# Four gated groups of a fused attention and expert kernel computed from seven block products instead of eight

## The chip, the cores and the metric

The kernel runs on one core of a Trainium2 chip. The metric is the device time of one execution in microseconds (us). TensorE (PE) multiplies matrices, VectorE (DVE) and ScalarE (ACT) work elementwise and can read PSUM, GpSimd (POOL) works elementwise on SBUF alone, and SyncE (SP) issues most transfers.

## The reference

Random-feature attention for 2 batches of 8 heads, then a gated product, then four experts weighted by probabilities. The part that the change touches is the gated product; x has 1152 rows (2 batches of 576) and 512 columns (d_model), w1 and w2 are 512 x 1024.

```python
def _moe_ref(x, w1, w2, w3, w_out):
    a = x @ w1
    b = x @ w2
    h = a * b @ w3
    return (h @ w_out).astype(np.float32)
```

The kernel folds w3 @ w_out into one 1024 x 512 matrix beforehand, so that the gated product is followed by one product with the folded matrix. The weights come as float64 and are turned into float32 on the chip. Each float32 operand is kept as two parts, high and low (`split`: ScalarE copies the high part, another engine subtracts it from the source), and a product is made of three passes, low by high, high by low and high by high (`PASSES`).

## The kernel before

Activations stand transposed: features on the partitions, tokens along the free dimension. `xb[kk]` (kk = 0 to 3) holds 128 features of x for both batches, high and low part, 1152 columns each. It is whole only when the attention of the last heads and of the 64 tail tokens of each batch has been placed.

The gated product goes by eight groups g of 128 hidden columns. `load_w12(g)` brings the group's columns of w1 and w2: a float64 block (`load_f64` on SP's queue), its conversion to float32 (`from_f64`: one ScalarE and two VectorE instructions, into one of two buffers `w12f`), and its split into one of eight 4 KB slots of the pool `w1` (ScalarE high, GpSimd low). Groups 0 and 1 are computed for each batch by itself (`gated`), groups 2 to 7 for both batches (`gated_both`): for w1 and then w2, three thirds of 384 columns, each 4 kk x 3 passes = 12 products into one PSUM bank. ScalarE copies the three banks of w1 to SBUF (`a2`), VectorE multiplies those of w2 onto them, and the product is split into the hidden tiles of the two batches.

The order around the change is written by hand in two strings. `BESIDE` puts the fold of w3 and w_out (`fold`) and the first groups beside the attention, `AFTER` lists what follows: `wN` is `load_w12(N)`, `bBG` is `gated` for batch B and group G, `mN` is `gated_both(N)`, `cB` is `expert_input(B)`, the product of the hidden tiles with the folded matrix. Within it the Tile framework's scheduler fixes each engine's queue when the kernel is built: an instruction goes in when its inputs are expected, earlier program text first. `tc.issue_after(ins)` keeps what follows behind `ins` on that engine. The queues are then worked off in order.

`fold` accumulates a 128 x 512 piece of the folded matrix in PSUM and splits it from there into `w3o` (high and low), in the pool `w3` beside `w1` on the right-hand side of SBUF. `expert_input(b)` multiplies by `w3o`: for each half c of 288 columns, four banks of 8 kk x 3 products each. For b = 1 it also makes the sums that the experts' own seven-product scheme wants (temporaries t1, t3, b22 in the pool `xq`). The experts (`hidden`, `sums`, `second`) already use that scheme: `NAMES` gives the seven pairs of operands, `ORDER` the order of the blocks for two halves X and Y, and `combine` makes the sums of the weights. Their first weights are loaded into the two tiles of the pool `raw`.

```python
PASSES = ((LO, HI), (HI, LO), (HI, HI))
ORDER = "X1 Y1 X5 Y5 X6 Y6 X2 X7 Y2 Y7 X3 X4 Y3 Y4".split()
NAMES = {
    "1": ("A11", "B11"), "2": ("A12", "B21"), "3": ("S4", "B22"), "4": ("A22", "T4"), "5": ("S1", "T1"), "6": ("S2", "T2"),
    "7": ("S3", "T3"),
}
```

Of the kernel before, what the change touches and what calls it, by code (L numbers as in the profile page):

```python
# [39 lines left out]


BESIDE = {1: 'o o o', 2: 'o o', 3: 'o o o f0', 4: 'f1 f2', 5: 'f3 f4', 6: 'f5 f67', 7: 'w0', 8: 'b00 w1'}
AFTER = 'w2 b01 w3 b10 w4 b11 w5 m2 w6 m3 w7 m4 m5 m6 m7 c0 c1'


@with_exitstack
def attention_moe_kernel(ctx: ExitStack, tc: tile.TileContext, q, k, v, omega, mw1, mw2, mw3, mwo, probs, ew1, ew2, out):
# [110 lines left out]
    w3_p = mctx.enter_context(tc.tile_pool(name="w3", bufs=1, side="right"))  # L158
    cctx = mctx.enter_context(ExitStack())
    cv = cctx.enter_context(tc.tile_pool(name="cv", bufs=2, side="right"))  # L160
    w12, hid, wo, w3o, x2, xf = {}, {}, [], [], {}, {}

    def gated_columns(src, g):
        return src[:, g * P:(g + 1) * P].rearrange("(k p) c -> p k c", p=P)

    def load_w12(g):

        for w, src in enumerate((mw1, mw2)):
            src = gated_columns(src, g)
            with ExitStack() as order:  # L170
                if g < EARLY:
                    f = next_block("w12f")
                else:
                    with tc.issue_after(pairs[-1].loaded):
                        r = load_f64(cv.tile([P, 512, 2], U32, tag="f64", name="f64", bufs=3), [src])
                    for ins in pairs[-1].split:
                        order.enter_context(tc.issue_after(ins))
                    f = from_f64(r, "w12f")
                t = load_w64(w1_p, f, "w12", nc.gpsimd)
            w12[w, g] = t.rearrange("p a (k c) -> p a k c", k=KD)  # L180

    def load_wo():

# [3 lines left out]
    def gated(a_p, bufs, b, g, tags):  # L187

        ht = hidden_tile(b, g)
        halves = []  # L190
        for w in range(2):
            bs = [bank(tags[2 * w + c]) for c in range(2)]
            for kk in range(KD):
                for n, (x, y) in enumerate(PASSES):
                    for c in range(2):
                        nc.tensor.matmul(
                            out=bs[c][:, :HS], lhsT=w12[w, g][:, x, kk], rhs=xt[b][kk][:, y, c * HS:(c + 1) * HS],
                            start=(kk == 0 and n == 0), stop=(kk == KD - 1 and n == 2),
                        )
            for c in range(2):  # L200
                if w == 0:
                    t = a_p.tile([P, HS], F32, tag="a", name="a", bufs=bufs)
                    nc.scalar.activation(out=t, in_=bs[c][:, :HS], func=ACTF.Copy)
                    halves.append(t)
                else:
                    t, s = halves[c], slice(c * HS, (c + 1) * HS)
                    nc.vector.tensor_tensor(out=t, in0=bs[c][:, :HS], in1=t, op=ALU.mult)
                    split(ht[:, HI, s], ht[:, LO, s], t)

    def hidden_tile(b, g):  # L210
        pool = (hx_p if g < HX_BUFS else h0_p) if b == 0 else h_p
# [3 lines left out]
    def gated_both(g):  # L215

        hts = [hidden_tile(b, g) for b in range(B)]
        third = B * S // 3
        cols = [slice(c * third, (c + 1) * third) for c in range(3)]
        tags = ALL_BANKS[0] + ALL_BANKS[1]  # L220
        kept = []
        for w in range(2):
            for c in range(3):
                ps = bank(tags[(g * 6 + w * 3 + c) % 8])
                for kk in range(KD):
                    for n, (x, y) in enumerate(PASSES):
                        nc.tensor.matmul(  # L227
                            out=ps[:, :third], lhsT=w12[w, g][:, x, kk], rhs=xb[kk][:, y, cols[c]],
                            start=(kk == 0 and n == 0), stop=(kk == KD - 1 and n == 2),
                        )  # L230
                if w == 0:
                    t = a_p.tile([P, third], F32, tag="a2", name="a", bufs=4)
                    nc.scalar.activation(out=t, in_=ps[:, :third], func=ACTF.Copy)
                    kept.append(t)
                else:
                    t = kept[c]
                    nc.vector.tensor_tensor(out=t, in0=ps[:, :third], in1=t, op=ALU.mult)  # L237
                    for b in range(B):
                        lo, hi = max(c * third, b * S), min((c + 1) * third, (b + 1) * S)
                        if lo < hi:  # L240
                            s = slice(lo - b * S, hi - b * S)
                            split(hts[b][:, HI, s], hts[b][:, LO, s], t[:, lo - c * third:hi - c * third])

    w3T = []
    for n in range(KF):
# [8 lines left out]
    def fold_transposed(u):  # L254

        r = next_block("w3f")
        t = cv.tile([P, 512], U32, tag="f64e", name="w3t", bufs=2).bitcast(F32)
        nc.vector.transpose(t, r.rearrange("p (j c g) -> p j g c", j=4, g=4))  # L260
        t = t.rearrange("p (j g r) -> p g j r", j=4, g=4)
        wt = cv.tile([P, 2, 512], F32R, tag="w3T", name="w3T", bufs=2)
# [6 lines left out]
    def fold(*ms):  # L269
# [3 lines left out]
        for u, (m, hf) in enumerate(UNITS):  # L273
# [7 lines left out]
                    start=(hf == 0 and n == 0), stop=(hf == 1 and n == 11),  # L281
                )
            if hf == 1:
                t = w3_p.tile([P, 2, 512], F32R, tag="w3o", name="w3o", bufs=KF)
                split(t[:, HI], t[:, LO], sums[m])
                w3o.append(t)

    def expert_input(b):

        for c in range(2):  # L290
            s = slice(c * HS, (c + 1) * HS)
            for i in range(KD):

                j = i // 2 + i % 2 * (KD // 2)
                ps = bank(ALL_BANKS[c][i])
                for kk in range(KF):
                    for n, (x, y) in enumerate(PASSES):
                        nc.tensor.matmul(
                            out=ps[:, :HS], lhsT=w3o[kk][:, x, j * P:(j + 1) * P], rhs=hid[b, kk][:, y, s],
                            start=(kk == 0 and n == 0), stop=(kk == KF - 1 and n == 2),  # L300
                        )
                p = ps[:, :HS]
                if b == 0:
                    if c == 0:
                        new_x2(("B11", "B21")[i % 2], i // 2)
# [369 lines left out]
    raw_p = ctx.enter_context(tc.tile_pool(name="raw", bufs=2, reuse_waits="tile"))  # L675
    h_p = mctx.enter_context(tc.tile_pool(name="h", bufs=KF, reuse_waits="tile"))
    h0_p = mctx.enter_context(tc.tile_pool(name="h0", bufs=KF - HX_BUFS, reuse_waits="tile"))
    a_p = cctx.enter_context(tc.tile_pool(name="a", bufs=1, reuse_waits="tile", side="right"))
    for s in AFTER.split():
        if s[0] == "w":  # L680
            load_w12(int(s[1]))
        elif s[0] == "c":
            if s == "c0":
                cctx.close()
                xq_p = mctx.enter_context(tc.tile_pool(name="xq", bufs=1, reuse_waits="tile", side="right"))
            expert_input(int(s[1]))
        elif s[0] == "m":
            gated_both(int(s[1]))
        else:
            gated(a_p, 4, int(s[1]), int(s[2]), ALL_BANKS[int(s[1])])  # L690
    mctx.close()
# [25 lines left out]
    turn = [0]  # L717
# [5 lines left out]
    def place(o, x, y, op):  # L723
        nc.vector.tensor_tensor(out=o, in0=x, in1=y, op=op)  # L724

    def parts(t, src):
        split(t[:, HI], t[:, LO], src)
        return t

    def combine(low, high, x11, x12, x21, x22, first, both):  # L730


        t = {}
        a = both(low)
        t["A11"], t["A12"] = a[0], a[1]
        t["A22"] = first(x22)
        place(x22, x21, x22, ALU.add)
        place(x21, x11, x21, ALU.subtract)
        a = both(high)
        t["S3"], t["S1"] = a[0], a[1]  # L740
        place(x11, x22, x11, ALU.subtract)
        place(x12, x12, x11, ALU.subtract)
        a = both(low)
        t["S2"], t["S4"] = a[0], a[1]
        return t

    def raw_half(pool, src):
        r = pool.tile([P, 2, 512], F32, tag="raw", name="raw")
# [20 lines left out]
    def load_w2(hf):  # L769
# [235 lines left out]
```

## Time and profile before

| | us |
|---|---|
| median of 3 runs | 654.55 |
| lowest, highest | 653.83, 654.69 |
| the profiled execution | 654.0 |
| its span, first to last instruction | 652.2 |
| TensorE busy in the span | 640.9 |
| VectorE busy | 458.9 |
| ScalarE busy | 415.8 |
| GpSimd busy | 122.2 |

All busy times are of the one profiled execution. Busy times of different engines overlap. A matmul's own duration is longer than the distance to the next one, since matmuls are pipelined; the distance is what adds up. The same holds in small for VectorE, whose next instruction can start up to 0.1 us before the one in front of it ends.

### The profile page before, as it was taken

To read this page: it belongs to the slowest core of one execution; us is meant where nothing else is said; L and a number is where in the kernel's file an instruction comes from. 1 tells how busy PE (TensorE), PEld (TensorE's weight loads), DVE (VectorE), ACT (ScalarE), POOL (GpSimd) and SP (SyncE) were. 2 spreads that over 40 slices of the span, in tenths; PEclk is the share of its full clock that TensorE was granted. 3 is DMA by queue.
4 is the path that set the end of the run, shared out by engine and by line. 5 is a ranking of instruction groups with operands and counts; after the bars stand their busy time and mean duration, and the time that the engine had idled before them with its cause. 6 is when DMAs were issued, how large, how long until landed. Compare 5 with 4: busy or idle time off the path is not lost.

```text
span 652.2 us, 12631 instructions
## 1 busy us (share of the span) xinstructions
PE 640.9 (98%) x4971; PEld 609.3 (93%) x4971; DVE 458.9 (70%) x756; ACT 415.8 (64%) x892; POOL 122.2 (19%) x145
## 2 busy tenths in 40 slices
PE   8998999999999999999999999999999999999997
PEld 6787787799999999999999999999999999999997
DVE  4678987957533261757958968788598679687795
ACT  5899556655522242457768767688677687687750
POOL 2223000133310000000131420430422413304200
PEclk9999999999999999999999999999999999999999
DMA  9978762136200011001244782881773855836824
GB/s 249 353 175 228 168 172 66 34 97 197 64 0 1 1 69 62 1 2 65 94 127 87 111 146 51 159 147 19 149 144 51 150 108 86 141 83 95 173 57 147
DMA packets 58396, 70.61 MB, mean 108 GB/s; under 512 B 8864, under 2 KB 43680, under 8 KB 58336
## 3 DMA queue, kind: packets, MB, share of 16 engines
q1 hardware_dynamic: 44720, 48.79, 25.6%
q0 software_dynamic: 12640, 20.19, 21.1%
q8 instruction: 39, 0.64, 0.4%
q10 hardware_dynamic: 976, 0.82, 0.4%
q14 instruction: 21, 0.17, 0.1%
HBM read 47.24 MB, written 22.54 MB: 107 GB/s over the span
## 4 chain that ended last, share of the span: by engine, by line
PE 88%; ACT 5%; DMA 3%; DVE 2%; issue 1%; SPq 1%; DVEq 0%; ACTq 0%
PE ps_f L828 7%; PE ps_f L913 6%; PE ps_et L828 3%; PE ps_po L828 3%; PE ps_w L828 3%; PE ps_x L828 3%; PE ps_kv L828 3%; PE ps_t L828 3%; PE ps_et L913 3%; PE ps_x L913 3%; PE ps_kv L913 3%; PE ps_w L913 3%; PE ps_t L913 3%; DMA f<-in_moe_w_dram 3%; PE ps_po L913 3%; PE ps_f L227 3%
## 5 line engine op out<-in xcount | busy, mean ns | idle before, releaser
L862 POOL DMA_DIRECT2D out_dram<-o x98 | 82.0, 935 | 352.5 <-DVE o L888 174.0
L84 DVE TENSOR_TENSOR hs<-hd,hs 128x1024 fp32r<-128x1024 f32 x48 | 58.4, 1219 | 0.8 <-ACT hs L83 0.8
L83 ACT ACTIVATE hs<-hd 128x1024 fp32r<-128x1024 f32 x48 | 50.6, 1055 | 7.6 <-PE ps_et L913 2.5
L828 PE MATMUL ps_f<-x,w1e 128*128 128x288 f32 x288 | 46.9, 294 | 0.0
L812 ACT ACTIVATE hd<-hd 128x288 f32<-128x288 f32 x96 | 40.9, 436 | 8.0 <-DVE hd L810 7.4
L724 DVE TENSOR_TENSOR hd<-hd 128x512 f32<-128x512 f32 x64 | 43.9, 686 | 1.5 <-ACT hd L812 0.4
L724 DVE TENSOR_TENSOR raw<-raw 128x512 f32<-128x512 f32 x64 | 43.9, 686 | 0.6
L84 DVE TENSOR_TENSOR w2e<-raw,w2e 128x1024 fp32r<-128x1024 f32 x32 | 38.8, 1218 | 6.1 <-ACT w2e L83 6.0
L913 PE MATMUL ps_f<-w2e,hs 128*128 128x256 f32 x288 | 42.7, 282 | 0.0
L828 PEld LDWEIGHTS ps_f<-x,w1e 128*128 128x128 f32 x288 | 41.1, 188 | 0.2
L913 PEld LDWEIGHTS ps_f<-w2e,hs 128*128 128x128 f32 x288 | 38.2, 191 | 0.1
L83 ACT ACTIVATE w2e<-raw 128x1024 fp32r<-128x1024 f32 x32 | 32.8, 1054 | 6.1 <-DVE raw L724 3.7
L84 POOL TENSOR_TENSOR w<-w12f,w 128x512 fp32r<-128x512 f32 x16 | 21.8, 1378 | 66.9 <-ACT w L83 59.2
L84 DVE TENSOR_TENSOR w1e<-raw,w1e 128x1024 fp32r<-128x1024 f32 x24 | 29.3, 1220 | 4.4 <-ACT w1e L83 4.3
L83 ACT ACTIVATE hid<-a 128x192 fp32r<-128x192 f32 (+2 forms) x32 | 13.4, 440 | 29.1 <-DVE a L237 25.2
L83 ACT ACTIVATE w1e<-raw 128x1024 fp32r<-128x1024 f32 x24 | 25.4, 1058 | 4.6 <-DVE raw L724 2.9
L279 PE MATMUL ps_po<-wo,w3T 128*128 128x512 f32 x96 | 24.1, 399 | 1.7 <-DVE w3T L84 1.7
L381 DVE TENSOR_REDUCE mx<-ps_f 128x4 f32<-128x512 f32 x24 | 16.5, 689 | 12.5 <-PE ps_f L375 11.5
L279 PE MATMUL ps_w<-wo,w3T 128*128 128x512 f32 x96 | 24.5, 400 | 0.6 <-DVE w3T L84 0.6
L885 ACT ACTIVATE o<-ps_f,pr 128x256 f32<-128x256 f32 (+1 forms) x37 | 17.8, 480 | 10.4 <-PE ps_f L913 9.6
L84 DVE TENSOR_TENSOR hid<-a,hid 128x192 fp32r<-128x192 f32 (+2 forms) x32 | 17.5, 563 | 9.0 <-ACT hid L83 9.0
L828 PE MATMUL ps_et<-x,w1e 128*128 128x288 f32 x144 | 23.6, 295 | 0.0
(307 smaller groups left out, 1711.5 us busy)
## 6 DMA issues: line engine op xcount, KB each, us to landing
raw<-in_moe_w_dram SPq DMA_DIRECT2D x32, 512.0 KB, 5.5
out_dram<-o POOLq DMA_DIRECT2D x56, 256.0 KB, 4.7
f<-in_moe_w_dram SPq DMA_DIRECT2D x64, 128.0 KB, 3.6
f<-in_moe_w_dram SPq DMA_DIRECT2D x16, 512.0 KB, 4.3
out_dram<-o POOLq DMA_DIRECT2D x42, 128.0 KB, 5.0
f<-in_moe_w_out_dram SPq DMA_DIRECT2D x8, 512.0 KB, 7.4
vr<-in_v_dram SPq DMA_DIRECT2D x8, 256.0 KB, 5.2
o<-out_dram SPq DMA_DIRECT2D x8, 256.0 KB, 4.8
```

The costliest lines, as they stand in the source:

```text
L83: high = nc.scalar.activation(out=hi, in_=src, func=ACTF.Copy)
L84: low = (eng or nc.vector).tensor_tensor(out=lo, in0=src, in1=hi.bitcast(F32), op=ALU.subtract)
L227: nc.tensor.matmul(out=ps[:, :third], lhsT=w12[w, g][:, x, kk], rhs=xb[kk][:, y, cols[c]], start=(kk == 0 and n == 0), stop=(kk == KD - 1 ...
L279: nc.tensor.matmul(out=sums[m], lhsT=w3T[u][:, a, g * P:(g + 1) * P], rhs=wo[hf * 4 + g][:, c], start=(hf == 0 and n == 0), stop=(hf == 1 ...
L381: top = nc.vector.tensor_reduce(out=mx, in_=pv, op=ALU.max, axis=AX.X, negate=True)
L724: nc.vector.tensor_tensor(out=o, in0=x, in1=y, op=op)
L812: nc.scalar.activation(out=h, in_=src, func=ACTF.Relu)
L828: nc.tensor.matmul(out=ps, lhsT=w1t[a][:, x, kk, g * P:(g + 1) * P], rhs=x2[b, kk][:, y, s], start=(k in "125" and kk == 0 and n == 0), st ...
L862: dma = nc.gpsimd.dma_start(out=out[toks, d], in_=src[rows], **({} if fresh else dict(accum_op=ALU.add))).ins
L885: nc.scalar.activation(out=o, in_=ps, func=ACTF.Copy, scale=pr[:, t, e:e + 1])
L913: nc.tensor.matmul(out=ps, lhsT=t[a][:, x, g, j * P:(j + 1) * P], rhs=w2t[b][:, y, g], start=(k in "15" and g == 0 and n == 0), stop=(k in ...
```

## The change

Groups 4 to 7 (`WINO = 4`) are computed by the same seven-product scheme as the experts. The blocks are: w1 and w2 as the two rows, the two halves of d_model as the inner index, and the two batches as the two columns. So a group has seven block products for each half of 288 columns, each block 2 kk x 3 passes = 6 products; the sums of blocks are accumulated in PSUM and, over SBUF tiles p1, p5 and p6, on VectorE; GpSimd makes one of the two products w1 by w2.

- `sums_of_x` makes T1, T2, T3 and the float32 form of T4 from xb, in eight steps (`tN` in `AFTER`: one step for each digit) that stand beside groups 1 to 3, and `last_sum_of_x` (`t9`) splits T4 into the second half of xb[0] and xb[1], behind group 3. The float32 T4 stands in the two tiles of the pool `raw` until then.
- `load_w12_sums` makes a group's weights by `combine`: four slots of the pool `w1` instead of two.
- `fold` keeps its result as float32 (VectorE copies it out of PSUM). `split_fold` (`s0`, `s1`) splits it later into slots of the pool `w1`, four tiles behind group 6 and four behind group 7.
- `expert_input(0)` goes in its first column half through kk 0 to 3 of all four banks and then through kk 4 to 7.
- The pools on the right-hand side change their order, and `a2` has three buffers instead of four.

The pieces of the diff that carry this (the functions `combine`, `place`, `parts` and the two tables only move up in the file):

```diff
-AFTER = 'w2 b01 w3 b10 w4 b11 w5 m2 w6 m3 w7 m4 m5 m6 m7 c0 c1'
+AFTER = 'w2 b01 t1 b10 w3 t12 b11 w4 t12 m2 t12 t1 m3 t9 w5 m4 w6 m5 w7 m6 s0 m7 s1 c0 c1'
+WINO = 4
...
+    def combine(low, high, x11, x12, x21, x22, first, both):
+        t = {}
+        a = both(low)
+        t["A11"], t["A12"] = a[0], a[1]
+        t["A22"] = first(x22)
+        place(x22, x21, x22, ALU.add)
+        place(x21, x11, x21, ALU.subtract)
+        a = both(high)
+        t["S3"], t["S1"] = a[0], a[1]
+        place(x11, x22, x11, ALU.subtract)
+        place(x12, x12, x11, ALU.subtract)
+        a = both(low)
+        t["S2"], t["S4"] = a[0], a[1]
+        return t
...
+    def load_w12_sums(g):
+        low, high = (gated_words(g, src) for src in (mw1, mw2))
+        (x11, x12), (x21, x22) = ((f[:, :256], f[:, 256:]) for f in (low, high))
+        def both(src):
+            t = load_w64(w1_p, src, "w12", nc.gpsimd)
+            return [t[:, :, k * 256:(k + 1) * 256].rearrange("p a (k c) -> p a k c", k=2) for k in range(2)]
+        def first(src):
+            t = w1_p.tile([P, 2, 512], F32R, tag=w1_p.name, name="w12")[:, :, :256]
+            split(t[:, HI], t[:, LO], src, eng=nc.gpsimd)
+            return t.rearrange("p a (k c) -> p a k c", k=2)
+        w12[g] = combine(low, high, x11, x12, x21, x22, first, both)
+
+    def sums_of_x(raw):
+        later = []
+        part, thirds = (h0_p.tile([P, 2, S], F32, tag=h0_p.name, name="xsum") for _ in range(2))
+        for kk in range(2):
+            x1, x2_ = xb[kk], xb[kk + 2]
...
+            def difference(o, p, q, eng):
+                sub(o, f32(*p, HI), f32(*q, HI), eng)
+                sub(o, o, f32(*p, LO), eng, ALU.add)
+                sub(o, o, f32(*q, LO), eng)
+            def less(o, p, q, eng):
+                sub(o, f32(*p, HI), q, eng)
+                sub(o, o, f32(*p, LO), eng, ALU.add)
+            f1, f2, f3 = part[:, 0], part[:, 1], thirds[:, kk]
+            difference(f1, (1, 1), (1, 0), nc.vector)
+            difference(f3, (2, 1), (1, 1), nc.gpsimd)
+            less(f2, (2, 1), f1, nc.vector)
+            f4 = raw_p.tile([P, 2, 512], F32, tag="raw", name="T4").rearrange("p a c -> p (a c)")[:, :S]
+            less(f4, (2, 0), f2, nc.gpsimd)
+            t1, t2, t3 = new(), new(), new()
+            later.append((t3, f3))
+            raw.append(f4)
...
+            yield
+            for t, f in ((t1, f1), (t2, f2)):
+                split(t[:, HI], t[:, LO], f)
+                yield
+        for t, f in later:
+            split(t[:, HI], t[:, LO], f)
+            yield
+
+    def last_sum_of_x(raw):
+        for kk in range(2):
+            t = xs["T4", kk] = xb[kk][:, :, S:]
+            split(t[:, HI], t[:, LO], raw[kk])
+
+    def gated_sums(g):
...
+        for o in ORDER:
...
+            for kk in range(2):
+                for n, (x, y) in enumerate(PASSES):
+                    nc.tensor.matmul(
+                        out=ps, lhsT=w12[g][a][:, x, kk], rhs=xs[b, kk][:, y, s],
...
+            if k in "156":
+                now["p" + k] = keep(k != "6", ps)
+            elif k == "2":
+                onto(now["p1"], ps)
+            elif k == "7":
+                onto(now["p5"], ps)
+            elif k == "3":
+                onto(now["p6"], ps)
+                onto(now["p6"], now["p5"], ALU.mult, nc.gpsimd)
+                put(1, s, now["p6"])
+            else:
+                onto(now["p1"], ps, ALU.mult)
+                put(0, s, now["p1"])
+
+    def split_fold(n):
+        for t in w3o[4 * n:4 * n + 4]:
+            w3s.append(load_w64(w1_p, t, "w3s", nc.vector))
...
-                t = w3_p.tile([P, 2, 512], F32R, tag="w3o", name="w3o", bufs=KF)
-                split(t[:, HI], t[:, LO], sums[m])
+                t = w3_p.tile([P, 512], F32, tag="w3o", name="w3o", bufs=KF)
+                nc.vector.tensor_copy(t, sums[m])
...
-            for i in range(KD):
+            halves = 2 if b == 0 and c == 0 else 1
+            banks = [bank(ALL_BANKS[c][i]) for i in range(KD)]
+            for i, hf in [(i, hf) for hf in range(halves) for i in range(KD)]:
...
+        elif s[0] == "t" and s != "t9":
+            with ExitStack() as order:
+                for ins in gone:
+                    order.enter_context(tc.issue_after(ins))
+                for n in s[1:]:
+                    next(steps)
...
-    w1e_p, hid_p, o_p, hq_p = right("w1e", 3), right("hid", 1), right("o", O_BUFS), right("hq", 2)
-    wt_p, r2_p, w2_p = right("wt", 2), right("r2", 2), right("w2e", 2)
-    hs_p, s_p = right("hs", HS_BUFS), right("s", 2)
+    hid_p, o_p, hq_p, s_p = right("hid", 1), right("o", O_BUFS), right("hq", 2), right("s", 2)
+    w1e_p, r2_p, w2_p, wt_p, hs_p = right("w1e", 3), right("r2", 2), right("w2e", 2), right("wt", 2), right("hs", HS_BUFS)
```

`gone` holds the two instructions of the last split of a hidden tile, so the steps `tN` go behind it on ScalarE and on VectorE.

## Rows read from the trace of the kernel before

**Rows 1.** The page: busy time of each engine, and TensorE's granted clock by slice.

```profile
PE 640.9 (98%) x4971; PEld 609.3 (93%) x4971; DVE 458.9 (70%) x756; ACT 415.8 (64%) x892; POOL 122.2 (19%) x145
...
PEclk9999999999999999999999999999999999999999
```

**Rows 2.** Stages: length, then each engine's busy us, clock, DMA share, GB/s.

```profile
154.00:184.00 30.00, 30.00 (x187) 30.00 (x186) 17.62 (x36) 15.36 (x33) 9.45 (x7) 1.00 0.22 70
...
184.50:235.20 50.70, 50.70 (x290) 50.70 (x289) 14.39 (x28) 13.18 (x29) 1.30 (x1) 1.00 0.00 1
```

**Rows 3.** Chain of waits from m3's end to the experts: start, us, what.

```profile
182.43 2.12 PE ps_po L227 x12
184.54 2.11 PE ps_t L227 x12
...
233.12 2.11 PE ps_po L227 x12
235.23 3.20 PE ps_t L298 x24
...
286.11 0.80 PE ps_f L828 x6
```

**Rows 4.** Low half on GpSimd (ns min/median/max); high half on ScalarE (busy, mean ns).

```profile
L84 POOL TENSOR_TENSOR wo<-wof,wo x8: 1264/1277/1411, 29.1 to 58.4; 128x512 fp32r<-128x512 f32 x8
...
L83 ACT ACTIVATE w<-w12f 128x512 fp32r<-128x512 f32 x16 | 10.0, 632 | 2.8 <-DVE w12f L121 1.2 <-PE ps_po L227 0.9 <-PE ps_po L196 0.7
```

**Rows 5.** VectorE in order of time: start, us, instruction.

```profile
146.00 0.45 DVE L84 TENSOR_TENSOR hid<-a,hid 128x288 fp32r<-128x288 f32 x1
146.37 0.68 DVE L121 SCALAR_TENSOR_TENSOR w12f<-w12f,f64e 128x512 uint32<-128x512 uint32 x1
146.97 1.51 DVE L120 TENSOR_SCALAR f64e<-f 128x512 uint32<-128x512 uint32 x1
...
154.35 0.23 DVE L84 TENSOR_TENSOR xt<-ps_et,xt 128x64 fp32r<-128x64 f32 x1
...
159.16 1.42 DVE L84 TENSOR_TENSOR hid<-a,hid 128x288 fp32r<-128x288 f32 x1
...
161.47 0.41 DVE L120 TENSOR_SCALAR f64e<-f 128x512 uint32<-128x512 uint32 x1
...
163.45 1.01 DVE L120 TENSOR_SCALAR f64e<-f 128x512 uint32<-128x512 uint32 x1 [0.96 <-DMA f<-in_moe_w_dram]
...
172.61 1.13 DVE L84 TENSOR_TENSOR hid<-a,hid 128x384 fp32r<-128x384 f32 x1 [0.59 <-ACT hid L83]
173.66 0.54 DVE L237 TENSOR_TENSOR a<-ps_po,a 128x384 f32<-128x384 f32 x1
174.13 1.32 DVE L121 SCALAR_TENSOR_TENSOR w12f<-w12f,f64e 128x512 uint32<-128x512 uint32 x1
175.37 0.55 DVE L84 TENSOR_TENSOR hid<-a,hid 128x384 fp32r<-128x384 f32 x1
...
183.45 0.63 DVE L84 TENSOR_TENSOR hid<-a,hid 128x192 fp32r<-128x192 f32 x2 [0.43 <-ACT hid L83]
...
239.77 2.13 DVE L724 TENSOR_TENSOR raw<-raw 128x512 f32<-128x512 f32 x3
```

**Rows 6.** GpSimd in order of time, the first of four pairs.

```profile
146.82 2.81 POOL L84 TENSOR_TENSOR w<-w12f,w 128x512 fp32r<-128x512 f32 x2 [2.94 <-ACT w L83]
```

**Rows 7.** SP's queue: the experts' first raw weights.

```profile
146.33 1.01 SPq L749 DMA_DIRECT2D raw<-in_moe_w_dram  x2
```

**Rows 8.** ScalarE and VectorE around the experts' start.

```profile
235.31 1.06 ACT L83 ACTIVATE w1e<-raw 128x1024 fp32r<-128x1024 f32 x1 [0.95 <-issue]
...
286.95 0.41 ACT L816 ACTIVATE p<-ps_f 128x288 f32<-128x288 f32 x1
...
288.58 0.46 DVE L324 TENSOR_TENSOR t<-xf,t 128x288 f32<-128x288 f32 x1
...
290.52 0.45 DVE L84 TENSOR_TENSOR x<-t,x 128x288 fp32r<-128x288 f32 x1
```

More of the change, by code (lines that the diff above doesn't have):

```diff
@@ new lines, in attention_moe_kernel, with place, parts @@
+    ft = fctx.enter_context(tc.tile_pool(name="ft", bufs=2, side="right"))
+    w12, hid, wo, w3o, w3s, x2, xf, xs = {}, {}, [], [], [], {}, {}, {}
+    turn = [0]
+    ORDER = "X1 Y1 X5 Y5 X6 Y6 X2 X7 Y2 Y7 X3 X4 Y3 Y4".split()
+    NAMES = {
+        "1": ("A11", "B11"), "2": ("A12", "B21"), "3": ("S4", "B22"), "4": ("A22", "T4"), "5": ("S1", "T1"), "6": ("S2", "T2"),
+        "7": ("S3", "T3"),
+    }
+    def place(o, x, y, op):
+        nc.vector.tensor_tensor(out=o, in0=x, in1=y, op=op)
+    def parts(t, src):
+        split(t[:, HI], t[:, LO], src)
+        return t
@@ L164, in gated_columns, with gated_words @@
         return src[:, g * P:(g + 1) * P].rearrange("(k p) c -> p k c", p=P)
+    def gated_words(g, src):
+        src = gated_columns(src, g)
+        if g < EARLY:
+            return next_block("w12f")
+        with ExitStack() as order:
+            with tc.issue_after(pairs[-1].loaded):
+                r = load_f64(cv.tile([P, 512, 2], U32, tag="f64", name="f64", bufs=3), [src])
+            for ins in pairs[-1].split:
+                order.enter_context(tc.issue_after(ins))
+            return from_f64(r, "w12f")
@@ L166, in load_w12 @@
     def load_w12(g):
+        if g >= WINO:
+            return load_w12_sums(g)
         for w, src in enumerate((mw1, mw2)):
[L169 to L179, printed above, removed]
@@ new lines, in last_sum_of_x, with new_bank, keep, onto @@
+    def last_sum_of_x(raw):
[3 more added lines that the diff above has]
+    def gated_sums(g):
+        hts = [hidden_tile(b, g) for b in range(B)]
+        tags = ALL_BANKS[0] + ALL_BANKS[1]
+        state = {}, {}
+        def new_bank():
+            turn[0] += 1
+            return bank(tags[turn[0] % 8])[:, :HS]
+        def keep(tag, src):
+            t = a_p.tile([P, HS], F32, tag="a", name="a", bufs=4) if tag else a_p.tile([P, B * S // 3], F32, tag="a2", name="a", bufs=3)[:, :HS]
+            nc.scalar.activation(out=t, in_=src, func=ACTF.Copy)
+            return t
+        def onto(t, src, op=ALU.add, eng=nc.vector):
+            eng.tensor_tensor(out=t, in0=src, in1=t, op=op)
+        def put(b, s, t):
+            split(hts[b][:, HI, s], hts[b][:, LO, s], t)
+        for o in ORDER:
+            c, k = "XY".index(o[0]), o[1]
+            s = slice(c * HS, (c + 1) * HS)
+            now = state[c]
+            if k in "125":
+                now[k] = new_bank()
+            ps = now["1" if k in "1674" else "5" if k in "53" else "2"]
+            a, b = NAMES[k]
+            for kk in range(2):
+                for n, (x, y) in enumerate(PASSES):
+                    nc.tensor.matmul(
+                        out=ps, lhsT=w12[g][a][:, x, kk], rhs=xs[b, kk][:, y, s],
+                        start=(k in "125" and kk == 0 and n == 0), stop=(k in "234" and kk == 1 and n == 2),
+                        skip_group_check=True,
+                    )
+            if k in "156":
[11 more added lines that the diff above has]
+                put(0, s, now["p1"])
@@ L241, in gated_both @@
                             s = slice(lo - b * S, hi - b * S)
[L242 removed]
+                            gone[:] = split(hts[b][:, HI, s], hts[b][:, LO, s], t[:, lo - c * third:hi - c * third])
     w3T = []
@@ L302, in expert_input @@
                 p = ps[:, :HS]
+                if hf < halves - 1:
+                    continue
                 if b == 0:
@@ L721, in next_bank @@
         return bank(("t", "f", "kv", "et", "f", "x", "w", "po")[turn[0] % 8])
[L723 to L745, printed above, removed]
     def raw_half(pool, src):
```

48 lines of the change are left out of this document (33 added, 15 removed).

## The prediction

> **What bounds the kernel now.** I read the page first: TensorE is busy 98% of the span and its clock is granted in full in all 40 slices [rows 1], so no term below comes from the clock. Then the table by stage: in the 50.7 us of the last four gated groups (m4 to m7) TensorE and its weight loads are busy for every microsecond, VectorE for 14.4 us, GpSimd for 1.3 [rows 2]. Then the chain of waits: from m4's first product to the folded product it is nothing but matmuls, end to end [rows 3]. So in this stage the number of products and their spacing set the end, and everything else is worth something only if it makes a product wait.
>
> **What the change removes.** m4 to m7 run from 184.54 to 235.23 us [rows 3]: 50.7 us for 4 x 72 products of 384 columns, 0.176 us each. The new form has 14 blocks of 6 products of 288 columns in a group, 4 x 84. Products of 288 columns stand 0.80 us for six, or 3.20 us for 24, in two other stages [rows 3]: 0.133 us each. 336 x 0.133 = 44.8 us. **Term 1: -5.9 us.** The other stage gives the same figure, so I keep no more than 0.5 us either way.
>
> **What it adds before m4: the sums of x.** x is whole only when the last tail is split, at 154.6 us [rows 5]. m4 starts at 184.5 and its third block (X5) wants T1, its fifth (X6) T2, its eighth T3, at 0.80 us a block: 186.1, 187.7 and 190.1. T4 can be split only when m3 has read xb for the last time, at 184.5, and X4 wants it at 193.3; two ScalarE and two VectorE passes of under 0.8 us fit. So the window for the sums is 154.6 to 187.6, 33.0 us. The reader should see that TensorE has nothing else to do if T2 is late: only X1, Y1, X2 and Y2 of a group need no sum.
>
> Work on VectorE in that window, by the spacing of starts in its order of time [rows 5]: 0.37 us for 288 columns, 0.60 for 512, so 0.67 for 576; a dependent chain of 512 columns is spaced (2.13 - 0.68) / 2 = 0.72, so 0.80 for 576.
> - Sums: per kk one chain of three (2 x 0.80 + 0.67) and one of two (0.80 + 0.67), 3.7; for both 7.5.
> - Low halves of T1, T2, T3 for both kk: 6 x 0.67 = 4.0.
> - w4's four places of 256 columns, 0.37 each: 1.5. w5's two float64 blocks, by the bit operations (0.41 and 0.68 less overlap): 1.9.
> - Hidden tiles that are there already: b10 and b11 4 x 0.37, m2 and m3 each 2 x 0.47 and 0.63 for two of 192 columns: 4.6.
> - Ten drains that read PSUM (four of 288, six of 384): 4.3.
> Together 23.8 us, 19.5 of it with all inputs in SBUF.
>
> Work on GpSimd: the nearest row is the 512-column subtraction, 1.28 us [rows 4], so 1.44 for 576. Ten sums 14.4, w4's four low halves 3 x 1.28 + 0.64 = 4.5, w5's first 1.3: 20.2 us. Each engine alone fits into 33.0.
>
> They don't run alone. While GpSimd subtracted from 146.82 on [rows 6], the bit operation on VectorE at 146.97 took 1.51 us instead of 0.41; so at 159.16, 163.45, 172.61 and 174.13, while the one at 173.66, which reads PSUM, took its ordinary 0.54 [rows 5]. From 154 to 184 the four lengthened ones add 0.97 + 0.60 + 0.58 + 0.64 = 2.8 us (against 0.45, 0.41, 0.55, 0.68) beside 9.45 us of GpSimd [rows 2]: **VectorE is held up for 0.30 of GpSimd's time**. That was with VectorE wanting SBUF for both inputs about 9.9 of 30 us (17.6 less 2.8, less eight PSUM drains and the small operations on the gate's weights), a third of the time; now it wants it 19.5 of 33.0. A GpSimd instruction meets a waiting one more often in that proportion: 0.30 x 0.59 / 0.33 = 0.54. The wait is 0.54 x 20.2 = 10.9, VectorE needs 23.8 + 10.9 = 34.7 us, T2 is 1.7 us late. **Term 2: +1.7 us.** The bounds: with the measured 0.30 nothing is late (29.9 us); with every GpSimd microsecond holding up VectorE, 44.0, it is 11.0 late. I stay near the row, scaled, because the scaling is what changes.
>
> The Trainium skill, page "SBUF — State Buffer", section "Who interferes with whom", has the rule: the second port pair of VectorE is GpSimd's, taken for a whole instruction, and whoever comes second stands still; an input from PSUM doesn't need it. The trace agrees, 1.51 us against 0.54. By the rule alone the sum below would come out at +1.2 instead of -3.8 us; that is the upper end of the second rival.
>
> **What it adds in m4 to m7.** VectorE: five float64 blocks 4.7, twelve places 4.5, sixteen hidden halves 5.9, T4 1.3, four fold splits 2.4, 32 PSUM drains 11.8: 30.6. GpSimd: weights 3.2 + 9.0, eight products of 288 columns 5.8: 18.0, holding up 7 us at the same scaling. 38 of 44.8 us: full, but not the bound. Weights: a group's chain is two conversions, then split, half split, two places, split, two places, split. ScalarE's split is 0.63 [rows 4] and GpSimd's 1.28, so the part behind the previous-but-one group's end (its A22 slot) is about 1.0 + 0.8 + 1.9 + 0.8 + 1.9 = 6.4 us against a group of 11.2. It costs nothing while VectorE keeps pace; if that cover goes, X5 of w5's or w6's group is the next late product. PSUM: six of eight banks a group, each asked for again 2.4 us or more behind its last reader. SP: the two raw tiles that hold expert weights from 146.33 on [rows 7] now hold T4 until m3's end; their next reader is at 235.31 [rows 8], 50 us later, so the transfer stays hidden, and it stands behind no float64 block that m5 wants.
>
> **The fold and its split.** Eight ScalarE passes leave the fold and VectorE copies 512 columns where it subtracted 512; nothing, within 0.5 us. Eight splits come back: four during m7, four behind it. The first column half now does 4 kk for four banks first, 48 x 0.133 = 6.4 us; four ScalarE passes and one low half behind them need about 4 x 0.63 + 0.7 = 3.2 and the last drains as much again. Zero.
>
> **The experts' start.** The tiles p1, p5 and p6 now lie among the first right-hand pools, where the last temporaries of the folded product (t, b) still live. ScalarE keeps p1 at 286.95 today, and VectorE's last read of t starts at 290.52, held by that queue; the operation before it starts at 288.58 [rows 8]. If p1 must wait, it comes near 290.1 and ends near 290.5, and X6 at 286.1 + 3.2 = 289.3 waits 1.3 us, unless X2 and Y2, which need nothing, are put first. Between 0 and 1.3: **term 3: +0.4 us.**
>
> **The sum** is -5.9 + 1.7 + 0.4 = -3.8 us. The profiled execution took 654.0 us (span 652.2), so 650.2; the median of the runs shown is 0.55 above it, so 650.8. What a measurement can tell from no change is about 0.2%, 1.3 us.
>
> **The rivals**, all in the held-up share of GpSimd's time, s, with lateness 20.2 s - 9.2:
> - *Fully covered*: s up to 0.46, T2 in time, experts' start filled: 654.0 - 5.9 = 648.1. For it: today's 0.30, and T3's halves need not precede T2's. Against it: double the demand.
> - *The gain is eaten*: s from 0.66 to 0.79, late by 4.2 to 6.8, for example 5.3 at 0.72: 653.8. If whatever reads SBUF twice on VectorE and all of GpSimd's work go strictly one after the other, 19.5 + 20.2 = 39.7 us, it is 6.7 late: 655.2. For it: the order at VectorE is fixed, so a low half of T2 stands behind m2's hidden halves whether they matter or not.
> - *Slower*: s above 0.79. VectorE becomes the bound in front of m4: its sums alternate with GpSimd's one for one, and the drains and hidden halves queue behind. At 0.9, 9.0 late: 654.0 - 5.9 + 0.4 + 9.0 = 657.5. For it: chains on both engines start at the same instant, 154.6. Against it: ten PSUM drains run beside GpSimd.
> - That the products don't shrink to 336 can't be: the order of blocks fixes their number.
>
> **How the numbers follow.** Forecast (s from 0.46 to 0.66, 648.1 to 652.7 or so) 0.42; fully covered 0.20; eaten 0.18; slower 0.20. The likeliest gives 650.8. Faster by over 0.2%: 0.62; within: 0.18; slower: 0.20. The range reaches from the covered case, less 0.3 for its spacing, 647.8, to 656.0, beyond which lies some 0.15 of the slower case; the forecast's own range is 648.1 to 653.3.
>
> **What would show it.** Right: 336 products of 288 columns at 0.133 us between m3 and the folded product; one gap on TensorE of 1 to 3 us before X5 or X6 of m4, ended by VectorE's low half of T1 or T2; VectorE instructions of 2 us beside GpSimd's sums. Wrong: no gap there (648), a gap over 6 us, gaps again at m5 or m6 that end at a weight's split, or a second one behind the folded product, at p1.

## The result and the profile after

The changed kernel takes 658.05 us (median of 4 runs, 657.71 to 660.27) against 654.41 before in the same comparison: a ratio of 1.0064, 95% interval 1.0041 to 1.0087 (worked out from all runs; the ratio of the two medians is 1.0056). It is slower by 0.6%, where 650.8 was forecast. Its profiled execution took 658.25 us, its span 656.5.

The page of the changed kernel, engines and TensorE's clock, answers to [rows 1]:

```profile
PE 638.0 (97%) x5019; PEld 604.4 (92%) x5019; DVE 504.8 (77%) x818; ACT 425.3 (65%) x920; POOL 157.5 (24%) x171
...
PEclk9999999999999999999999999999999999999999
```

48 more products, all of them smaller, give TensorE 2.9 us less to do; VectorE has 45.9 us more, GpSimd 35.3. The stages show where the time went, with the columns of [rows 2]:

```profile
150.00:160.00 10.00, 7.57 (x52) 7.02 (x51) 10.00 (x17) 1.99 (x6) 6.72 (x4) 1.00 0.34 106
160.00:170.00 10.00, 10.00 (x67) 10.00 (x66) 9.82 (x11) 3.84 (x9) 9.23 (x7) 1.00 0.01 2
...
180.00:190.00 10.00, 8.82 (x54) 8.50 (x53) 10.00 (x14) 4.60 (x9) 5.20 (x5) 1.00 0.00 0
190.00:200.00 10.00, 6.74 (x36) 6.07 (x35) 9.32 (x17) 6.78 (x16) 2.93 (x2) 0.83 0.50 157
200.00:210.00 10.00, 10.00 (x78) 10.00 (x77) 8.53 (x16) 5.70 (x14) 6.36 (x6) 1.00 0.01 2
```

VectorE is full from 150 us to m4, and TensorE stands in three places. TensorE in order of time (the bracket is the idle time before it and what ended it) names them:

```profile
155.02 0.53 PE L359 MATMUL ps_po<-xt,w 128*128 128x288 f32 x2 [0.38 <-DVE xt L85]
...
159.07 1.82 PE L359 MATMUL ps_et<-xt,w 128*128 128x288 f32 x12 [2.05 <-DVE prs L883]
...
185.90 2.38 PE L392 MATMUL ps_po<-xt,w 128*128 128x384 f32 x12 [1.18 <-DVE a L402]
188.12 0.96 PE L321 MATMUL ps_kv<-xt,w 128*128 128x288 f32 x6
...
192.17 1.07 PE L321 MATMUL ps_et<-xt,w 128*128 128x288 f32 x6 [0.31 <-DVE a L402]
196.05 1.78 PE L321 MATMUL ps_kv<-T,w 128*128 128x288 f32 x6 [2.81 <-ACT a L302]
197.62 0.68 PE L321 MATMUL ps_w<-xt,w 128*128 128x288 f32 x2
198.10 1.54 PE L321 MATMUL ps_f<-T,w 128*128 128x288 f32 x6
...
200.01 0.96 PE L321 MATMUL ps_f<-xt,w 128*128 128x288 f32 x6
```

First, 2.4 us in groups 0 and 1, which wait for the last tails of x (the second bracket names the small reduction that stands right behind the last tail in VectorE's queue). Second, m3's last bank, 1.2 us, because a drain of PSUM is late. Third, m4. Its first product starts at 188.12, where the kernel without the sums (the first experiment) starts it at 183.77: 4.35 us late. In that kernel, the same view:

```profile
183.77 0.96 PE L305 MATMUL ps_kv<-xt,w 128*128 128x288 f32 x6
```

And m4's first 48 products in the changed kernel end at 200.01, 11.9 us where 48 x 0.133 = 6.4 would do; then blocks stand 0.80 apart and nothing waits until the experts. Of these 5.5 us, 3.1 are waits. The 18 products between 196.05 and 200.01 take 3.96 us instead of 2.4, and the clock granted from 190 to 200 is 0.83, a part of that stretch at the lower of the two levels: behind the wait of 2.81 us the first six products take 1.57 us (196.05 to 197.62) where six ordinarily take 0.80, and in the table of stages cut to single microseconds the clock is 0.50 from 196 to 199. That loses 1.6 us; the remaining 0.8 us lies in small pieces around the two waits. Behind the wait of 2.05 us the clock stayed at 1.00.

What held m4 up is not T2. The chain of waits in front of 196.05, in order of time:

```profile
189.09 0.67 DVE T L85
189.76 0.47 DVE hid L85
190.23 1.42 DVE w12f L175
191.65 0.48 DVE a L402
...
192.15 0.53 ACT hid L84
...
193.89 0.56 DVE a L402
...
194.47 0.62 ACT hid L84 x2
195.09 0.52 ACT w L84
195.61 0.30 ACT a L302
```

The low halves of T1, T2 and T3 are all done at 189.8. X6 goes on adding into the PSUM bank of X1, so it waits for p1, the copy of that bank that `keep` makes on ScalarE (L302), and ScalarE's queue stands behind m3's hidden tiles, which stand behind m3's drains on VectorE (L402, at 191.65 and 193.89), which stand behind everything that the sums delayed.

Why VectorE is late is seen where it works beside GpSimd. VectorE in order of time, changed kernel:

```profile
153.22 1.61 DVE L247 TENSOR_TENSOR xsum<-xsum,xt 128x576 f32<-128x576 f32 x1
...
155.22 1.69 DVE L85 TENSOR_TENSOR hid<-a,hid 128x288 fp32r<-128x288 f32 x1
156.84 1.95 DVE L247 TENSOR_TENSOR xsum<-xsum,xt 128x576 f32<-128x576 f32 x1
158.71 0.21 DVE L85 TENSOR_TENSOR xt<-ps_et,xt 128x64 fp32r<-128x64 f32 x1
...
160.60 1.40 DVE L884 TENSOR_SCALAR prs<-prs 128x9 f32<-128x9 f32 x1
```

The same instructions where GpSimd does nothing (the last experiment below, same view):

```profile
153.75 0.74 DVE L247 TENSOR_TENSOR xsum<-xsum,xt 128x576 f32<-128x576 f32 x1
...
155.55 0.44 DVE L85 TENSOR_TENSOR hid<-a,hid 128x288 fp32r<-128x288 f32 x1
155.92 0.74 DVE L247 TENSOR_TENSOR xsum<-xsum,xt 128x576 f32<-128x576 f32 x1
156.59 0.21 DVE L85 TENSOR_TENSOR xt<-ps_et,xt 128x64 fp32r<-128x64 f32 x1
...
158.15 0.16 DVE L884 TENSOR_SCALAR prs<-prs 128x9 f32<-128x9 f32 x1
```

A sum goes from 0.74 to 1.6 or 1.95 us, and an instruction on nine columns from 0.16 to 1.40: each ends soon after the GpSimd instruction that runs when it starts. GpSimd in order of time, changed kernel:

```profile
156.56 1.61 POOL L247 TENSOR_TENSOR xsum<-xt,xt 128x576 f32<-128x576 f32 x1
158.13 3.83 POOL L247 TENSOR_TENSOR xsum<-xsum,xt 128x576 f32<-128x576 f32 x2
```

GpSimd's sum from 156.56 ends at 158.17 and VectorE's from 156.84 at 158.79; GpSimd's pair from 158.13 ends at 161.96 and the nine columns from 160.60 at 162.00. That VectorE waits for GpSimd, and doesn't only end beside it, is what the experiment with the idle subtractions shows. What VectorE's instructions from 150 to 190 us have over their ordinary lengths adds up to 16.0 us, beside 24.8 us of GpSimd up to 188: a held-up share of 0.65.

### The profile page after: what moved, and what is told of

The parts are those of the page before. It is cut to its first block, busy times and chain, and to the rows that moved or that the text cites. A ratio compares the mean times of both kernels' runs of the same rounds, so it can differ in the third digit from the quotient of the medians.

```text
span 656.5 us, 12870 instructions
## 1 busy us (share of the span) xinstructions
PE 638.0 (97%) x5019; PEld 604.4 (92%) x5019; DVE 504.8 (77%) x818; ACT 425.3 (65%) x920; POOL 157.5 (24%) x171
## 4 chain that ended last, share of the span: by engine, by line
PE 76%; DVE 11%; ACT 4%; DMA 4%; issue 3%; SPq 1%; POOL 0%; DVEq 0%; ACTq 0%
PE ps_f L980 7%; PE ps_f L1065 6%; PE ps_et L980 3%; PE ps_w L980 3%; PE ps_x L980 3%; PE ps_po L980 3%; PE ps_t L980 3%; PE ps_kv L980 3%; PE ps_et L1065 3%; PE ps_kv L1065 3%; PE ps_t L1065 3%; PE ps_x L1065 3%; PE ps_w L1065 3%; PE ps_po L1065 3%; DMA f<-in_moe_w_dram 2%
## 5 line engine op out<-in xcount | busy, mean ns | idle before, releaser
L85 POOL TENSOR_TENSOR w<-w12f,w 128x512 fp32r<-128x512 f32 (+1 forms) x24 | 32.4, 1360 | 64.9 <-ACT w L84 61.8
L444 PE MATMUL ps_w<-wo,w3T 128*128 128x512 f32 x96 | 24.4, 401 | 0.4 <-DVE w3T L85 0.4
L84 ACT ACTIVATE hid<-a 128x288 fp32r<-128x288 f32 (+2 forms) x32 | 13.8, 439 | 15.9 <-POOL a L306 5.6
L980 PE MATMUL ps_w<-x,w1e 128*128 128x288 f32 x144 | 23.6, 295 | 0.3 <-ACT o L1037 0.3
```

Of the source, the lines that this page charges most:

```text
L84: high = nc.scalar.activation(out=hi, in_=src, func=ACTF.Copy)
L85: low = (eng or nc.vector).tensor_tensor(out=lo, in0=src, in1=hi.bitcast(F32), op=ALU.subtract)
L444: nc.tensor.matmul(out=sums[m], lhsT=w3T[u][:, a, g * P:(g + 1) * P], rhs=wo[hf * 4 + g][:, c], start=(hf == 0 and n == 0), stop=(hf == 1 ...
L980: nc.tensor.matmul(out=ps, lhsT=w1t[a][:, x, kk, g * P:(g + 1) * P], rhs=x2[b, kk][:, y, s], start=(k in "125" and kk == 0 and n == 0), st ...
```

## The experiments

Theory L (lock): what the sums of x cost is the time that VectorE stands still for GpSimd; the sums themselves would fit. Rival W (work): VectorE has too much to do in front of m4, wherever the sums run. Further rivals: the smaller products, the weights' chain or the fold cost more than forecast.

**No sums.** T1 to T4 become views of x, so the kernel leaves out the sums and their splits; everything else stays.

```diff
-            difference(f3, (2, 1), (1, 1), nc.gpsimd)
...
-            xs["T1", kk], xs["T2", kk], xs["T3", kk] = t1, t2, t3
+            xs["T1", kk] = xs["T2", kk] = xs["T3", kk] = xs["T4", kk] = x1[:, :, S:]
```

> The changed kernel without the sums of x: T1 to T4 are views of x itself, so the seven-block products, the weights' sums, the fold's late split and the pools stay and only the sums and their splits are left out. Theory (the sums on VectorE and GpSimd displace the tail splits of x and the drains in VectorE's queue): TensorE has no gap over 0.5 us between 150 and 200 us, and the time is that of before less the product saving, 648 to 649.5. Rival (the weights' chain with four slots and four places holds up m4): a gap of 3 us or more stays in front of m4's X6, and the time stays at 653 or above. Rival (fold, pools, folded product): the gaps go and the time still stays above 651.

Measured: 648.38 us (648.25 to 648.41), ratio 0.9912 (0.9899 to 0.9926), and no idle TensorE between 130 us and the experts. Products, weights and fold deliver what was forecast; all that is lost is lost to the sums. The first product of the experts, in the changed kernel and in this one, TensorE in order of time:

```profile
289.07 0.96 PE L980 MATMUL ps_f<-x,w1e 128*128 128x288 f32 x6
```

```profile
279.23 0.96 PE L964 MATMUL ps_f<-x,w1e 128*128 128x288 f32 x6
```

**The rest alone.** The old product for all groups, with the new pools, fold and fold's split.

```diff
-WINO = 4
+AFTER = 'w2 b01 w3 b10 w4 b11 w5 m2 w6 m3 w7 m4 m5 m6 s0 m7 s1 c0 c1'
+WINO = 8
```

> Everything of the change but the seven-block products: groups 4 to 7 in their old form, no sums, with the fold's float32 result, its late split, the halves of the folded product and the new order of pools. Theory: nothing but the fold's 0.4 us, 653.7 to 654.7. Rival (fold, pools, folded product): slower than before by 1.5 us or more, 656 and above.

Measured: 654.59 (654.2 to 655.29), ratio 1.0008 (1.0000 to 1.0017): no change. Inside it two small things cancel. TensorE's waits behind the experts' start (who waited for whom: us in total, times, longest) are, here as in the changed kernel:

```profile
PE ps_t L1065 <- ACT hd L964: 1.1, 1, 1.1
PE ps_w L980 <- ACT o L1037: 0.3, 1, 0.3
```

Before, one wait of 0.58 us stood there: 0.9 us more, 27 and 37 us into the experts (a third wait of 0.2 us is in both kernels); from their first product to the end they take 1.2 us longer (366.3 before, 367.4 here). And m4 starts at 183.92 instead of 184.38 in TensorE's order of time: the stages up to there give 0.5 us back, and TensorE's waits in the fold fall from 2.3 to 1.8 us.

**Sums on VectorE.** The ten sums that GpSimd made go to VectorE, 6.7 us of work more for the fuller engine. Here L and W part.

```diff
-            difference(f3, (2, 1), (1, 1), nc.gpsimd)
+            difference(f3, (2, 1), (1, 1), nc.vector)
...
-            less(f4, (2, 0), f2, nc.gpsimd)
+            less(f4, (2, 0), f2, nc.vector)
```

> The changed kernel with all ten GpSimd sums (f3 and f4 of both kk) moved to VectorE. If what costs is VectorE being held up while GpSimd subtracts: VectorE gains ten instructions of 0.67 us (6.7 us) and loses about 0.65 of 14.4 us of hold-up (9.4 us), so the time is the same or up to 3 us below the changed kernel, 655 to 658.5. If VectorE's plain amount of work is what costs and the hold-up is small: 6.7 us more in front of m4, 662 to 666.

Measured: 650.0 (649.61 to 650.37), ratio 0.9937 (0.9923 to 0.9950): faster than before by 0.6%, below what I had expected of either theory. W falls. L's direction holds, its size was put too small: 8.0 us come back where I had 3 at most. The table by stage of this kernel:

```profile
150.00:190.00 40.00, 40.00 (x257) 39.92 (x257) 39.15 (x75) 21.78 (x49) 11.41 (x9) 1.00 0.20 62
190.00:200.00 10.00, 10.00 (x76) 9.82 (x75) 9.96 (x18) 4.58 (x12) 7.05 (x6) 1.00 0.36 124
```

VectorE is as full as in the changed kernel, 39.15 of 40 us against 39.72, but it gets through 75 instructions instead of 55, and TensorE never waits here.

**Three groups, more time.** Only groups 5 to 7 take the new form; m4 gives the sums one group more.

```diff
-WINO = 4
+AFTER = 'w2 b01 w3 b10 w4 b11 t1 m2 t12 w5 t12 m3 t12 t1 m4 t9 w6 m5 w7 m6 s0 m7 s1 c0 c1'
+WINO = 5
```

> Seven-block products for groups 5 to 7 alone; group 4 in its old form, and the sums of x one place later in the order, so that they have 12.7 us more. Theory: the product saving is 3 x 1.47 = 4.4 us, VectorE has room (its queue was full from 150 to 196), the tail splits are no longer behind sums; 650 to 652. Rival (weights' chain): the same gap at m5, 655 and above.

Measured: 655.99 (655.85 to 657.39), ratio 1.0037 (1.0024 to 1.0049); 4 us above the range of the theory, and in that of the rival. The tails come in time now, but in front of the first new group TensorE waits as before. TensorE in order of time:

```profile
199.78 1.38 PE L321 MATMUL ps_kv<-xt,w 128*128 128x288 f32 x6 [3.19 <-ACT a L398]
```

The rival's number came, but not its mechanism: this wait ends with m4's copy on ScalarE, which frees a bank, and not with a split of weights. The clock is 0.83 again from 200 to 210 us. In both places tried the sums take their toll, so the price isn't a deadline for T2 alone.

**Sums behind the tails.** The sums may start only when all of x is placed.

```diff
-                for ins in gone:
+                for ins in (*gone, *placed):
```

> The changed kernel with its sums on VectorE and ScalarE kept behind the last split of x's tails in those engines' queues. Theory (GpSimd's sums hold VectorE up, and its queue has no room from 150 to 196 us): TensorE's wait of 2 us for the tails at 157 goes, but the same work comes later, the waits at m3's end and at m4's X6 grow, and the time stays within 1 us of the changed kernel, 657 to 659. Rival (only the place of the sums in front of the tails costs): 2.4 us or more less, 655.6 or below.

Measured: 659.4 (658.03 to 659.68), ratio 1.0077 (1.0065 to 1.0089), 0.4 us above the range expected and 1.4 above the changed kernel; the rival falls. The waits mostly move: 1.4 us instead of 2.4 at the tails, 4.1 instead of 2.8 at X6. TensorE in order of time:

```profile
155.45 1.82 PE L359 MATMUL ps_et<-xt,w 128*128 128x288 f32 x12 [1.42 <-DVE xt L85]
...
195.92 1.78 PE L321 MATMUL ps_kv<-T,w 128*128 128x288 f32 x6 [4.08 <-ACT a L302]
```

**Idle subtractions.** Sums on VectorE, and twelve GpSimd subtractions whose result nobody reads.

```diff
+            for _ in range(6):
+                nc.gpsimd.tensor_tensor(out=room[:, S:], in0=f32(1, 0, HI)[:, :448], in1=f32(2, 0, HI)[:, :448], op=ALU.subtract)
```

> All sums on VectorE as in the fast version, and 12 GpSimd subtractions of 448 columns added at the place of the old ones, which read two parts of x in SBUF and write columns that nobody reads (about 13 us of GpSimd). Theory (a GpSimd instruction that reads SBUF holds VectorE up): back to 655 to 659. Rival (the chains between VectorE and GpSimd were the cost, the waits of one for the other's sums): within 1 us of the fast version, 649 to 651.

Measured: 661.67 (661.03 to 661.84), ratio 1.0115 (1.0102 to 1.0128), 11.7 us above the same kernel without them and 2.7 above the range expected. No instruction reads their result, and the first low half of weights behind the ten starts 0.81 us after them, waiting for ScalarE, so it isn't GpSimd's own queue that is late: the cost comes from GpSimd being at work beside VectorE. A part of it is TensorE's clock, 0.91 over the 40 us from 150 and 0.72 from 199 to 205, which is 3.6 and 1.7 us at most. The two engines of this kernel in order of time:

```profile
151.89 1.40 DVE L85 TENSOR_TENSOR hid<-a,hid 128x288 fp32r<-128x288 f32 x1
153.21 1.68 DVE L247 TENSOR_TENSOR xsum<-xt 128x576 f32<-128x576 f32 x1
154.81 0.21 DVE L85 TENSOR_TENSOR xt<-ps_et,xt 128x64 fp32r<-128x64 f32 x1
154.94 1.24 DVE L121 TENSOR_SCALAR f64e<-f 128x512 uint32<-128x512 uint32 x1
```

```profile
151.38 15.12 POOL L271 TENSOR_TENSOR T<-xt,xt 128x448 f32<-128x448 f32 x10
```

Ten GpSimd instructions in 15.1 us, and in between VectorE gets in one at a time; whatever length it has alone (0.41 to 0.74), it takes 1.2 to 1.7. Of the lines shown only the tail, which reads one input from PSUM, keeps its 0.21. L stands.

**Idle fills.** The same with thirty fills, which read nothing.

```diff
+            for _ in range(15):
+                nc.gpsimd.memset(room[:, S:], 0.0)
```

> The same as with the idle subtractions, but with 30 GpSimd fills of 448 columns in their place, which only write (about 14 us of GpSimd). Theory (what holds VectorE up is GpSimd reading SBUF): 649.5 to 651. Rival (a busy GpSimd queue, late low halves of the weights, or any use of SBUF by GpSimd is enough): 653 and above, close to the run with the idle subtractions.

Measured: 12 runs in two groups, four from 651.21 to 652.01 and eight from 657.62 to 661.54; the ratio, 1.0033 (0.9997 to 1.0070), describes neither group. Even the short ones lie above the range of the theory, and the long ones are where the rival has them. The profiled execution (660.09) shows one thing that I had not expected, VectorE and GpSimd in order of time:

```profile
150.14 0.68 DVE L122 SCALAR_TENSOR_TENSOR w12f<-w12f,f64e 128x512 uint32<-128x512 uint32 x1
...
151.11 0.75 DVE L247 TENSOR_TENSOR xsum<-xt 128x576 f32<-128x576 f32 x1
...
151.91 9.72 DVE L121 TENSOR_SCALAR f64e<-f 128x512 uint32<-128x512 uint32 x1
```

```profile
149.71 11.65 POOL L271 MEMSET T<- 128x448 f32 x28
```

Two-input instructions run at their ordinary 0.68 and 0.75 us beside the fills, but the one-input bit operation (0.41 alone) stands for 9.72 us until the 28 fills are through, and TensorE behind it for 8.57. So the theory of this run, that only a GpSimd instruction that reads SBUF holds VectorE up, falls for this kind of instruction. The Trainium skill, page "SBUF — State Buffer", section "Who interferes with whom", says that a two-input VectorE instruction collides with a GpSimd instruction that reads SBUF and not with one that only writes, and that a one-input scalar operation can take both ports and then does collide; this trace agrees with both, 0.75 us against 9.72. The four short runs have no profile; that the bit operation got in ahead of the fills there is only likely.

**The product on VectorE too.** Sums on VectorE, and `onto(p6, p5, mult)`.

```diff
-                onto(now["p6"], now["p5"], ALU.mult, nc.gpsimd)
+                onto(now["p6"], now["p5"], ALU.mult)
```

> The fast version with the gated product of the second batch (p6 by p5, eight instructions of 288 columns) on VectorE too. Theory: VectorE gains eight times 0.37 us and loses up to eight times 0.8 us of hold-up in m4 to m7, where TensorE waits for 0.6 us in all: 649.3 to 650.3, no more than 0.7 below the fast version. Rival (VectorE's amount of work is the bound in m4 to m7): above 651.

Measured: 649.12 (649.05 to 649.35), ratio 0.9926 (0.9914 to 0.9938), 0.2 us below the range of the theory; the rival falls. In m4 to m7 TensorE is idle for 0.14 us, between 200 and 210.

**Half the sums on GpSimd, two ways.** Only `less(f4, ...)`, four subtractions, or only `difference(f3, ...)`, six, is left there.

```diff
-            difference(f3, (2, 1), (1, 1), nc.gpsimd)
+            difference(f3, (2, 1), (1, 1), nc.vector)
```

> The changed kernel with the six three-term subtractions (f3) on VectorE and only the four two-term ones (f4) left on GpSimd, about 5.8 us of GpSimd instead of 14.4. Theory A (what the sums cost is GpSimd's time beside a busy VectorE, dose by dose): between the two ends already timed, 650.0 with no sum on GpSimd and 658.05 with all ten, at the shorter end: 652 to 654. Theory B (one of the two chains is decisive, because VectorE waits for its result in its own queue or the low half of T3 stands in front of T2's): this one or its mirror image is at 650 and the other at 658.

> The mirror image: f4 on VectorE and the six subtractions of f3 left on GpSimd, about 8.6 us of GpSimd. Theory A: above the run with f4 there, 653.5 to 656. Theory B: 650 or 658, whichever the mirror image is not.

Measured: with the four 652.87 (651.23 to 655.1), ratio 0.9983 (0.9972 to 0.9993); with the six 654.2 (653.78 to 654.69), ratio 1.0001 (0.9992 to 1.0009). Both lie in the ranges of theory A, between 650.0 and 658.05, so neither chain alone decides. The profiled execution of the first was one of its shortest, 651.39.

**The weights on VectorE too.** In addition the low halves of the weights of groups 4 to 7.

```diff
-            t = load_w64(w1_p, src, "w12", nc.gpsimd)
+            t = load_w64(w1_p, src, "w12", nc.vector)
...
-            split(t[:, HI], t[:, LO], src, eng=nc.gpsimd)
+            split(t[:, HI], t[:, LO], src, eng=nc.vector)
```

> All sums and the products on VectorE, as in the version at 649.1, and in addition the low halves of the weights of the last four groups on VectorE instead of GpSimd, so that GpSimd does nothing between 154 us and the folded product. GpSimd loses about 18 us of work, VectorE gets 28 instructions of 0.4 to 0.6 us, some 10 to 11 us, 2.4 of it in front of m4. Theory A (GpSimd's time is what VectorE loses): 648.4 to 649.6, the remaining waits in front of m4 shorter. Rival (VectorE's own work is now the bound: 44 to 46 us in 44.8 us of m4 to m7): 650.5 to 654 with TensorE waiting behind VectorE's weights in m5 to m7.

Measured: 648.5 (648.24 to 648.86), ratio 0.9914 (0.9902 to 0.9927): the lowest median, 0.9% faster than before, and within its interval the time without any sums at all; its interval also overlaps that of the version in front of it (0.9914 to 0.9938). From 150 to 190 us VectorE is busy for 39.97 us of the 40, and TensorE still never waits there, nor until the experts. Two stages of it:

```profile
180.00:190.00 10.00, 10.00 (x70) 10.00 (x69) 10.00 (x22) 7.46 (x17) 0.00 (x0) 1.00 0.15 52
190.00:200.00 10.00, 10.00 (x77) 10.00 (x77) 8.38 (x20) 5.06 (x11) 0.00 (x0) 1.00 0.33 107
```

Put together, by GpSimd's busy time from 150 to 190 us (the table by stage of each profiled execution):

| on GpSimd | GpSimd busy, us | median, us |
|---|---|---|
| nothing | 0.3 | 648.5 |
| weights | 11.5 | 649.1 |
| weights, products | 11.4 | 650.0 |
| weights, products, four sums | 17.2 | 652.9 |
| weights, products, six sums | 19.1 | 654.2 |
| all, as changed | 24.9 | 658.05 |

Beyond the 11 us of the weights each microsecond of GpSimd costs about half a microsecond of the kernel and a little more towards the end: (652.9 - 650.0) / 5.8 = 0.50, (654.2 - 650.0) / 7.7 = 0.55, (658.05 - 650.0) / 13.5 = 0.60. These are averages of one kernel, not a rate: the 11 us of the weights cost about 0.6, and the idle subtractions, which stand back to back, cost 11.7 us for 24.4 - 11.4 = 13.0, or 0.90 each, part of it by the clock. The products run behind 190 us and so don't show in the column; the medians come from several comparisons, in which the kernel before had 653.93 to 654.41, so steps of under half a microsecond say nothing.

## Why the prediction was wrong

**Term 1** was right: 336 products of 288 columns, 0.80 us a block. From m4's first product to the experts' first it is 101.6 us before (184.38 to 285.95 in TensorE's order of time; the chain of [rows 3] has both 0.16 later) and 95.5 without sums (183.77 to 279.23): 6.1 us less, where 5.9 was forecast.

**Term 2, the sums of x, is the step that failed.** Forecast 1.7 us. The experts start at 289.07 in the changed kernel and at 279.23 without the sums: 9.8 us, 4.35 in front of m4 (2.4 at the tails, 1.2 at m3's bank, the rest in small pieces) and 5.5 in it. Two things in it were off.
- The held-up share was scaled to 0.54 and came out at 0.65. By the prediction's own formula that is 20.2 x 0.65 - 9.2 = 3.9 us, 2.2 more. (The 16.0 us held up in all, counted over a longer stretch, would make 6.8.)
- The larger part: the formula priced one deadline, T2's low half. VectorE works its queue off in order, and the sums stand in it ahead of things that other engines want sooner: the last tails of x, the drains that free PSUM banks, m3's hidden halves, and through those ScalarE's copy p1. The forecast let the sums start at 154.6, behind the last tail; VectorE's second sum starts at 153.22, and the last tail is split at 158.71. T2 was there by 189.8 at the latest, m4's start had slipped to 188.12, and X6 started six microseconds after that, when p1 had been copied. The gap of 1 to 3 us in front of X6 that the prediction names as a sign of being right was there, 2.81 us, but T2 did not end it. In place of 3.9 us stand 8.2, and the clock's 1.6 us behind the wait, which the prediction ruled out from [rows 1], come on top: 9.8.

**The rival** on the other side, that VectorE's sums alternate with GpSimd's one for one and the drains and hidden halves queue behind, is what happened, at 658.05 for a forecast of 657.5. Its condition, a share above 0.79, was wrong for the same reason: 0.65 was enough, because more than T2 hung on it. That its number came so near is partly luck: its example took a share of 0.9 and had no clock term, and 1.6 of the 9.8 us are the clock's.

**Against "fully covered"**: the work does fit, but only on one engine. That VectorE's own 23.8 us fit into the window was borne out (with 6.7 us more of it all sums together cost 1.6 us, 648.4 to 650.0); I took GpSimd's 20.2 us as help beside it, and they were the cost.

**Term 3** was mis-sized and misplaced: no wait at p1 (the experts' first blocks stand 0.80 us apart), but 1.2 us more in the experts, 0.9 of it waits 27 and 37 us later, in the kernel without the new product as well; 0.4 was forecast. Why ScalarE's order comes out worse there with the new pools wasn't tried. **Weights, fold, its split and SP**: nothing, as forecast, but for 0.6 us that the stages with the fold give back (m4 at 183.77 without sums, instead of 184.38).

The sum as measured: -6.1 + 9.8 + 1.2 - 0.6 = +4.3 us, and the spans differ by 656.5 - 652.2 = 4.3.

## What to carry to other kernels

Elementwise work with SBUF inputs that is moved to GpSimd beside a busy VectorE can cost more than it relieves: here ten sums took 16.4 us of GpSimd and cost 8 us of kernel more than on VectorE, where they are 6.7 us of work and all sums together cost 1.6 of kernel. It isn't so at every place: the weights' 11 us on GpSimd cost about 0.6. Price such work on an in-order queue by everything that stands behind it, not by the one result that the change adds, and look first for what the queue frees for others (PSUM banks, tails of an operand). Where the sum of terms leaves TensorE a wait of some microseconds, look whether the rows show a lower clock behind such a wait, and add it.

## What the hardware showed that was not expected

- One VectorE instruction can be held for many GpSimd instructions in a row: 9.72 us behind back-to-back fills, where a share "of GpSimd's time" suggests one at a time. Behind subtractions it was one at a time, 1.2 to 1.7 us each.
- GpSimd can be slow beside VectorE as well: in the run with the idle subtractions one low half of weights, 512 columns, which [rows 4] has at 1.28 us, took 3.23 us at 194.61, while VectorE ran one two-input instruction behind the other. That VectorE held it up there wasn't tested.
- A tiny instruction is held like a large one: nine columns, 1.40 us instead of 0.16.
- TensorE's clock, granted in full in the whole kernel before, fell to 0.83 over 10 us behind waits of 2.81, 3.19 and 4.08 us, and cost 1.6 us behind the first of them. With the idle subtractions it was 0.50 from 156 to 162 us, behind a wait of 2.37 us; behind the wait of 2.05 us in the changed kernel it stayed at 1.00.
